# Forgetting attention and SwiGLU FFN on one core: stage-by-stage merged order against an order made by a planner

## Chip, cores and metric

One NeuronCore of one Trainium2 chip. The metric is the device time of one execution in microseconds; the kernel before takes 549.05 us (median of three runs, 547.57 to 549.45).

The engines' short names: PE (TensorE, matmul; PEld its weight loads), DVE (VectorE), ACT (ScalarE), POOL (GpSimd), SP (SyncE, which here only issues DMAs). Each engine executes its own instructions strictly in the order in which the program lists them, and waits on semaphores for the others; so the written order decides what stands behind a wait.

## What is computed

Eight batches, eight heads, 576 tokens, head width 64; then an FFN on all 4608 tokens with model width 512 and hidden width 1536. Everything is float32 outside; the matmuls run in bf16.

```python
def _attn_ref(q, k, v, f):
    scores = (1 / np.sqrt(D)) * q @ k.T              # per batch and head
    cum = np.cumsum(np.log(np.clip(f, 0.0001, 1.0)), axis=-1)
    scores = np.where(causal, -1e9, scores + cum[..., :, None] - cum[..., None, :])
    attn = np.exp(scores - scores.max(-1))
    attn = attn / (attn.sum(-1) + 1e-09)
    return attn @ v

def _moe_ref(x, w_gate, w_val, w_out):               # x: heads side by side
    g = x @ w_gate
    return (g * sigmoid(g) * (x @ w_val)) @ w_out
```

The row term of the decay cancels in the softmax, so the kernel only needs `cum` of the keys.

## The kernel before

**Attention** works on 32 head pairs (two heads of a batch fill the 128 partitions). Queries are cut into nine blocks of 64 tokens; block i sees 64(i+1) keys.

For each pair: `load_pair` (L121) loads q and k on SP's queue so that each packet is one row of 64 elements; q is laid out block-diagonally (zeros in the other head's half), k in six pieces of 96 rows. `cast` (L156) makes bf16 on POOL, `transposes` (L173) turns the nine q and six k pieces with 128-column PE transposes into two PSUM banks `tt`, and DVE copies them out to `kt` and `qz`. `scores` (L205) makes for each block one or two score matmuls (L235), a mask matmul on its last 64 columns (L238), one DVE operation that adds `cb` (the cumulative decay, read back from DRAM for each pair) and finds the minimum (L242), and one ACT exponential that also sums (L247). `normalize` (L253) takes reciprocals on DVE (L261, L262) and multiplies on POOL into a packed bf16 tile `pk` (L267), in three groups of blocks (0 to 3, 4 to 7, 8); a DMA transpose on SP's queue turns each group of `pk` into `pT` (L271). `weighted` (L278) multiplies the values of both heads, as one 128-column weight, with `pT` for both heads (L292): of each result only the half that belongs to the head is copied, by two ACT copies of 64 partitions, from the one PSUM bank `xo` into the ring `xT` (L305). The values come through casting DMAs on POOL's queue (L152), the FFN weights too (L403, L407).

**FFN** works on nine tiles of 512 tokens. A gate unit (`gate`, L312) is four matmuls of 512 columns with `wg` (`gp`), a tanh on ACT (L329), four matmuls with `wv` (`vp`), and two DVE products (L333, L337) into `hh`; twelve of them make a tile. A projection unit (`project`, L341) is twelve matmuls (L349) for 128 tokens, an ACT scaling (L353) and an output DMA. `gp`, `vp` and `op` share three PSUM banks; scores have two, `tt` two, `xo` one.

**Order.** It is written by hand: stage s of 33 merges, by fractions of the stage, the scores of pair s, the weighted sums of pair s - 1, the transposes of pair s + 1, the casts of pair s + 2, the loads of pair s + 3 (`merge`, L359), and from stage five on four FFN units. What is left of the FFN follows after the last stage. In the first stages the weights are loaded at one piece a stage (L399).

Of the kernel before, what the change touches and what calls it, by code (L numbers as in the profile page):

```python
# [8 lines left out]
F32 = mybir.dt.float32  # L9
# [3 lines left out]
AX = mybir.AxisListType  # L13
# [3 lines left out]
HUGE = 3.0e38  # L17


@with_exitstack  # L20
def kernel(
# [16 lines left out]
    P = 128  # L38
# [6 lines left out]
    MT = 512  # L45
    NMT = N_TOK // MT
    scale = 1.0 / (D ** 0.5)
    assert NB * QB == S and D == 64 and NMT * MT == N_TOK
# [5 lines left out]
    GCH = [2, 4, 5]  # L54
    GOFF = [0, 8, 24]
    NSLOT = 29

    ORDER = [8, 4, 5, 6, 7, 0, 1, 2, 3]
    KR, KC = 96, 6
    NRING = 5 * MT  # L60

    consts = ctx.enter_context(tc.tile_pool(name="consts", bufs=1))
    keep = ctx.enter_context(tc.tile_pool(name="keep", bufs=1))
    ldb = ctx.enter_context(tc.tile_pool(name="ldb", bufs=2))
    att = ctx.enter_context(tc.tile_pool(name="att", bufs=2))
    cpool = ctx.enter_context(tc.tile_pool(name="cpool", bufs=2))
    tpool = ctx.enter_context(tc.tile_pool(name="tpool", bufs=3))
    epool = ctx.enter_context(tc.tile_pool(name="epool", bufs=4))
    small = ctx.enter_context(tc.tile_pool(name="small", bufs=4))
    ptpool = ctx.enter_context(tc.tile_pool(name="ptpool", bufs=2))  # L70
    ffn = ctx.enter_context(tc.tile_pool(name="ffn", bufs=2))
    spool = ctx.enter_context(tc.tile_pool(name="spool", bufs=3))
    opool = ctx.enter_context(tc.tile_pool(name="opool", bufs=2))
    ps = ctx.enter_context(tc.tile_pool(name="ps", bufs=1, space=PSUM))


    ident = consts.tile([P, P], BF16)
    make_identity(nc, ident[:, :])


    maskf = consts.tile([P, QB], F32)
# [6 lines left out]
    mask = consts.tile([P, QB], BF16)  # L88
    nc.vector.tensor_copy(mask, maskf)

    xT = consts.tile([P, KD, NRING], BF16)
    wg = consts.tile([P, KD, DF], BF16)
    wv = consts.tile([P, KD, DF], BF16)
    wo = consts.tile([P, KF, DM], BF16)


    qfs, kfs, vts, pks = [], [], [], []
    for n in range(2):
        qf = keep.tile([P, NB, 2, D], F32, name=f"qf{n}")
        nc.vector.memset(qf[0:64, :, 1, :], 0.0)  # L100
        nc.vector.memset(qf[64:128, :, 0, :], 0.0)
        qfs.append(qf)
        kf = keep.tile([P, KC, 2, D], F32, name=f"kf{n}")
        nc.vector.memset(kf[KR:P, :, :, :], 0.0)
        kfs.append(kf)
        vt = keep.tile([P, 5, H, D], BF16, name=f"vt{n}")
        nc.gpsimd.memset(vt[64:128, 4, :, :], 0.0)
        vts.append(vt)

        pk = keep.tile([P, NSLOT, P], BF16, name=f"pk{n}")  # L110
        nc.gpsimd.memset(pk[:, 4:6, :], 0.0)
        nc.gpsimd.memset(pk[:, 20:22, :], 0.0)
        pks.append(pk)

    evs = {}
    for i in range(0, NB, 2):
        ev = keep.tile([P, QB * (i + 2)], F32, name=f"ev{i}")
        nc.gpsimd.memset(ev[:, QB * (i + 1):], 0.0)
        evs[i] = ev

    st = {}  # L121


    def load_pair(p):
        b, hp = divmod(p, NPB)
        qf, kf = qfs[p % 2], kfs[p % 2]

        def lq(h):
            return lambda: nc.sync.dma_start(
                out=qf[64 * h:64 * h + 64, :, h, :],  # L130
                in_=q[b, 2 * hp + h].rearrange("(j r) d -> r j d", r=64),
            )

        def lk(h):
            return lambda: nc.sync.dma_start(
                out=kf[0:KR, :, h, :],
                in_=k[b, 2 * hp + h].rearrange("(c r) d -> r c d", r=KR),
            )
        return [lq(0), lq(1), lk(0), lk(1)]

    def load_cum(p):
        cb = cpool.tile([P, S], F32, name="cb")
        for h in range(2):
            nc.sync.dma_start(
                out=cb[64 * h:64 * h + 64, :],
                in_=cum_dram[2 * p + h:2 * p + h + 1, :].to_broadcast((64, S)),
            )
        st["cb", p] = cb

    def load_v(b, c):  # L150
        n = min(P, S - P * c)
        nc.gpsimd.dma_start(  # L152
            out=vts[b % 2][0:n, c, :, :],
            in_=v[b, :, P * c:P * c + n, :].rearrange("h p d -> p h d"),
        )


    def cast(p):

        def cq():  # L160
            qb = ldb.tile([P, NB, P], BF16, name="qb")
            nc.gpsimd.tensor_scalar(
                qb, qfs[p % 2].rearrange("r j h d -> r j (h d)"), -scale, 1.0,
                op0=ALU.mult, op1=ALU.mult)
            st["qb", p] = qb

        def ck():
            kb = ldb.tile([P, KC, P], BF16, name="kb")
            nc.gpsimd.tensor_copy(kb, kfs[p % 2].rearrange("r j h d -> r j (h d)"))
            st["kb", p] = kb  # L170
        return [cq, ck]

    def transposes(p):  # L173

        def start():
            st["kt", p] = att.tile([P, S], BF16, name="kt")
            st["qz", p] = att.tile([P, NB, P], BF16, name="qz")

        def one(bank, j):
            def f():  # L180
                if j == 0:
                    st["tt"] = ps.tile([P, 8, P], BF16, name="tt", tag="tt", bufs=2)
                tt = st["tt"]
                n = 8 * bank + j
                src = st["kb", p][:, n, :] if n < KC else st["qb", p][:, n - KC, :]
                nc.tensor.transpose(tt[:, j, :], src, ident)  # L186
            return f

        def evac(bank):
            tt = st["tt"]  # L190
            if bank == 0:
                nc.vector.tensor_copy(st["kt", p].rearrange("p (c k) -> p c k", k=KR),
                                      tt[:, 0:KC, 0:KR])
                nc.vector.tensor_copy(st["qz", p][:, 0:2, :], tt[:, KC:8, :])
            else:
                nc.vector.tensor_copy(st["qz", p][:, 2:9, :], tt[:, 0:7, :])

        def both(*fs):
            def f():
                for x in fs:  # L200
                    x()
            return f

        steps = []
        for n in range(15):  # L205
            bank, j = divmod(n, 8)
            fs = [one(bank, j)]
            if n == 0:
                fs.insert(0, start)
            if n in (7, 14):  # L210
                fs.append(lambda bank=bank: evac(bank))
            steps.append(both(*fs))
        return steps

    def scores(p):

        def begin():
            st["tm", p] = small.tile([P, NB + 1], F32, name="tm")
            st["ls", p] = small.tile([P, NB], F32, name="ls")
            st["rl", p] = small.tile([P, NB], F32, name="rl")  # L220

        def block(i):
            def f():
                if i == ORDER[0]:
                    begin()
                kt, qz, cb = st["kt", p], st["qz", p], st["cb", p]
                tm, ls = st["tm", p], st["ls", p]
                L = QB * (i + 1)
                tt = tpool.tile([P, S], F32, name="t")
                n0 = min(L, 512)  # L230
                parts = [(0, n0)] + ([(512, L)] if L > 512 else [])
                for n, (a, z) in enumerate(parts):
                    last = z == L
                    sp = ps.tile([P, 512], F32, name="sp", tag="sp", bufs=2)
                    nc.tensor.matmul(sp[:, :z - a], qz[:, i, :], kt[:, a:z],  # L235
                                     start=True, stop=not last)
                    if last:
                        nc.tensor.matmul(sp[:, z - a - QB:z - a], ident, mask,  # L238
                                         start=False, stop=True)
                    init = HUGE if n == 0 else tm[:, NB:NB + 1]  # L240
                    acc = tm[:, i:i + 1] if last else tm[:, NB:NB + 1]
                    nc.vector.tensor_tensor_reduce(  # L242
                        out=tt[:, a:z], in0=sp[:, :z - a], in1=cb[:, a:z], scale=1.0,
                        scalar=init, op0=ALU.add, op1=ALU.min, accum_out=acc,
                    )
# [6 lines left out]

    def normalize(p, g):  # L253

        i0, i1 = GROUPS[g]
        w = i1 - i0
        pk = pks[p % 2]

# [233 lines left out]
```

## Time and profile before

| what | value |
|---|---|
| median of 3 runs | 549.05 us |
| profiled execution: span from first to last instruction | 546.6 us |
| PE, DVE, ACT, POOL busy | 79%, 64%, 57%, 48% of the span |
| first FFN matmul | 94.2 us |
| start of the last stretch, FFN alone | about 461 us |
| mean granted TensorE clock | 0.928 |

The profile is one execution. "Busy" is the time in which an engine has at least one instruction under way; idle time is put down to what released the engine. A group's row gives its line, engine, operation, output and inputs, shapes, count, busy time, mean duration, and the idle time ahead of it with its releaser. Matmul ends are modelled, so the spacing of starts in a dense run says more of PE's rate than a matmul's duration. A few per cent of matmul records are missing. Shares of DMA time can exceed 1, since packets of a queue overlap.

### The profile page before, as it was taken

What the parts mean: (1) busy time and instruction counts of PE and PEld (TensorE: products, weight loads), DVE (VectorE), ACT (ScalarE), POOL (GpSimd) and SP (SyncE); (2) the same over time, 40 slices, a digit from 0 to 9 for tenths busy, and PEclk for the clock granted to TensorE, in tenths of its full rate; (3) what the DMA queues carried; (4) which work ended last, traced back from release to release, by engine and by line L of the source; (5) the groups of instructions that cost most, each with busy time, mean ns of one, the idle gap of its engine ahead of it and who ended that gap; (6) DMA issues with size and microseconds to landing.
All of it is one profiled execution on the core that took longest, in us unless ns stands there. A gap on an engine that the chain in (4) does not pass through costs nothing.

```text
span 546.6 us, 9410 instructions
## 1 busy us (share of the span) xinstructions
PE 433.7 (79%) x2684; PEld 226.4 (41%) x2736; DVE 352.0 (64%) x1154; ACT 314.0 (57%) x915; POOL 264.1 (48%) x424
## 2 busy tenths in 40 slices
PE   1423516877598888888888888889888988999997
PEld 1312314434344444444444444444444443444443
DVE  6622516767777777777777777777777776454450
ACT  2432626655667766667677667777776766333321
POOL 8561826546655565556555655565556533000000
PEclk9855656989789999999999999999999999999999
DMA  9899999997998999989989989999989754110102
GB/s 140 158 175 147 190 107 181 179 171 137 174 171 170 158 179 149 184 164 153 181 164 164 170 164 165 165 168 168 171 169 171 117 129 117 43 40 38 40 19 96
DMA packets 248403, 78.51 MB, mean 144 GB/s; under 512 B 236960, under 2 KB 238496, under 8 KB 248352
## 3 DMA queue, kind: packets, MB, share of 16 engines
q1 hardware_dynamic: 208096, 68.48, 63.2%
q0 software_dynamic: 40256, 9.44, 19.5%
q8 instruction: 21, 0.34, 0.3%
q14 instruction: 30, 0.25, 0.2%
HBM read 47.33 MB, written 9.58 MB: 104 GB/s over the span
## 4 chain that ended last, share of the span: by engine, by line
PE 56%; DVE 12%; ACT 9%; issue 7%; DMA 7%; POOL 2%; SPq 2%; DVEq 0%; ACTq 0%; POOLq 0%
PE op L349 15%; PE gp L320 13%; PE vp L320 10%; PE xo L292 8%; DMA pT<-pk 6%; PE sp L235 5%; DVE t L242 5%; DVE hh L337 4%; PE tt L186 3%; ACT xT L305 3%; ACT e L247 3%; DVE u L333 2%; ACT th L329 2%; ACT ev L247 2%; PE sp L238 1%
## 5 line engine op out<-in xcount | busy, mean ns | idle before, releaser
L267 POOL TENSOR_SCALAR pk<-ev,rl 128x640 bf16<-128x640 f32 (+4 forms) x160 | 93.0, 581 | 194.3 <-ACT ev L247 73.8
L242 DVE CUSTOM_DVE_ANT_0 t<-sp,cb 128x512 f32<-128x512 f32 (+7 forms) x288 | 134.5, 476 | 80.5 <-PE sp L238 54.2
L292 PE MATMUL xo<-pT,vt 128*128 128x128 bf16 (+2 forms) x348 | 104.4, 304 | 78.0 <-ACT xT L305 46.3
L247 ACT ACTIVATE e<-t,tm 128x384 f32<-128x384 f32 (+3 forms) x128 | 71.3, 557 | 109.1 <-DVE tm L242 62.7
L320 PE MATMUL vp<-xT,wv 128*128 128x512 bf16 x412 | 120.5, 380 | 1.6 <-DVE u L333 0.7
L320 PE MATMUL gp<-xT,wg 128*128 128x512 bf16 x416 | 119.9, 383 | 2.1 <-ACT xT L305 1.6
L333 DVE SCALAR_TENSOR_TENSOR u<-th,gp 128x512 f32<-128x512 f32 x108 | 74.1, 686 | 57.9 <-ACT th L329 57.9
L349 PE MATMUL op<-wo,hh 128*128 128x512 bf16 x420 | 110.2, 379 | 0.4
L247 ACT ACTIVATE ev<-t,tm 128x576 f32<-128x576 f32 (+4 forms) x160 | 89.3, 558 | 33.2 <-DVE tm L242 26.7
L235 PE MATMUL sp<-kt,qz 128*128 128x512 bf16 (+4 forms) x320 | 93.5, 308 | 18.2 <-DVE tm L242 16.6
L329 ACT ACTIVATE th<-gp 128x512 f32<-128x512 f32 x108 | 63.4, 587 | 45.8 <-PE gp L320 38.3
L337 DVE TENSOR_TENSOR hh<-u,vp 128x512 bf16<-128x512 f32 x108 | 74.3, 688 | 11.3
L292 PEld LDWEIGHTS <-vt 128*128 128x128 bf16 x352 | 36.2, 103 | 81.8 <-issue 42.7
L267 POOL TENSOR_SCALAR pk<-e,rl 128x384 bf16<-128x384 f32 (+3 forms) x128 | 67.5, 527 | 0.0
L186 PE MATMUL tt<-ident,qb 128*128 128x128 bf16 x288 | 61.1, 239 | 1.1 <-issue 0.9
L305 ACT CAST xT<-xo 64x256 bf16<-64x256 f32 (+1 forms) x192 | 59.2, 308 | 4.3 <-PE xo L292 2.3
L238 PE MATMUL sp<-mask,ident 128*128 128x64 bf16 x288 | 57.6, 202 | 0.0
L186 PEld LDWEIGHTS <-qb 128*128 128x128 bf16 x288 | 30.5, 108 | 56.2 <-issue 39.0
L235 PEld LDWEIGHTS <-qz 128*128 128x128 bf16 x320 | 33.0, 103 | 40.5 <-issue 9.1
L238 PEld LDWEIGHTS <-ident 128*128 128x128 bf16 x288 | 29.6, 103 | 44.4 <-issue 28.4
L320 PEld LDWEIGHTS <-wg 128*128 128x128 bf16 x432 | 36.1, 98 | 27.3 <-issue 2.8
L320 PEld LDWEIGHTS <-wv 128*128 128x128 bf16 x432 | 35.5, 98 | 24.9 <-issue 8.3
(41 smaller groups left out, 402.2 us busy)
## 6 DMA issues: line engine op xcount, KB each, us to landing
qf<-in_q_dram SPq DMA_DIRECT2D x64, 144.0 KB, 4.4
kf<-in_k_dram SPq DMA_DIRECT2D x64, 144.0 KB, 3.4
cb<-cum_f SPq DMA_DIRECT2D x64, 144.0 KB, 3.6
out_dram<-ot SPq DMA_DIRECT2D x36, 256.0 KB, 2.7
vt<-in_v_dram POOLq DMA_DIRECT2D x32, 128.0 KB, 4.8
pT<-pk SPq DMA_TRANSPOSE x96, 3.9
wg<-in_moe_w_gate_dram POOLq DMA_DIRECT2D x4, 384.0 KB, 9.1
wv<-in_moe_w_val_dram POOLq DMA_DIRECT2D x4, 384.0 KB, 11.0
```

Source lines behind the costliest of these rows:

```text
L186: nc.tensor.transpose(tt[:, j, :], src, ident)
L235: nc.tensor.matmul(sp[:, :z - a], qz[:, i, :], kt[:, a:z], start=True, stop=not last)
L238: nc.tensor.matmul(sp[:, z - a - QB:z - a], ident, mask, start=False, stop=True)
L242: nc.vector.tensor_tensor_reduce(out=tt[:, a:z], in0=sp[:, :z - a], in1=cb[:, a:z], scale=1.0, scalar=init, op0=ALU.add, op1=ALU.min, accu ...
L247: nc.scalar.activation(e[:, :L], tt[:, :L], AF.Exp, bias=tm[:, i:i + 1], scale=-1.0, accum_out=ls[:, i:i + 1])
L267: nc.gpsimd.tensor_scalar(pg[:, 0:m, i - i0, :], e[:, :P * m].rearrange("p (c k) -> p c k", k=P), rl[:, i:i + 1], 1.0, op0=ALU.mult, op1=A ...
L292: nc.tensor.matmul(xo[:, lo * P:w * P], vt[:, c, 2 * hp:2 * hp + 2, :].rearrange("p h d -> p (h d)"), pT[:, c * w + lo:(c + 1) * w, :].rea ...
L305: nc.scalar.copy(dst, xo4[r, :, h, :])
L320: nc.tensor.matmul(st[name], w_[:, ko, fc * P:(fc + 1) * P], xT[:, ko, x0:x0 + MT], start=(ko == 0), stop=(ko == KD - 1))
L333: nc.vector.scalar_tensor_tensor(u, st["th"], 1.0, st["gp"], op0=ALU.add, op1=ALU.mult)
L337: nc.vector.tensor_mul(st["hh", t][:, fc, :], u, st["vp"])
L349: nc.tensor.matmul(op, hh[:, fc, ms * P:(ms + 1) * P], wo[:, fc, :], start=(fc == 0), stop=(fc == KF - 1))
```

## The change

The hand-merged stages are replaced by a planner that runs while the program is built. Every piece of work is declared as an operation: the engines that may do it with a duration for each, what it reads and writes, a priority. `Plan.order` then repeatedly takes the operation that can start first (by priority where several can), gives it a buffer, and moves that engine's clock on; the program is written in order of these starts. Buffers of a ring are given out in order of priority, so that a later user cannot overtake an earlier one. Copies out of PSUM may go to ACT or DVE as the plan finds them free.

Beside the order itself, these things differ:

- q and k: a partition holds 8 (q) or 6 (k) neighbouring rows of a head, so 72 and 96 partitions are used, and a packet is 2 KB or 1.5 KB. Transposes are 72 and 96 columns wide, 14 a pair instead of 15. The copy out of PSUM restores the order of tokens: it reads with a stride and writes `kt` in order; `qz` is written with a stride.
- Weighted sums: two groups (blocks 0 to 3, 4 to 8) instead of three; each key chunk is two matmuls with 64 value columns, one a head, which write partitions 0 to 63 and 64 to 127 of `xo`; one 128-partition copy follows instead of two.
- The packed weights have 25 slots a pair instead of 29. For the first six pairs they are transposed on TensorE, in banks of the FFN's ring (`gv`), and copied by ACT or DVE; the other 26 pairs use the DMA transpose.
- The first four pairs get `cb` by loading the gates with a broadcast and summing them on 128 partitions; the others read `cum_f` back from DRAM. Their groups of blocks 0 to 3 come first, for all four pairs.
- Values are loaded in float32 on SP's queue and cast on POOL. FFN weights come in column cuts (256, 256, 512, 512), each waiting for the one two before it.
- FFN tiles: 256, 256, seven of 512, 256, 256 tokens. In a 256-token tile a PSUM bank holds two hidden chunks. `op` has a bank of its own, `tt` has one instead of two; scores keep two, `xo` one, `gv` three.

The core of the diff:

```diff
+class Plan:
+    def order(self):
...
+        while ready:
+            best = None
+            for n, r in ready.items():
+                o = self.ops[n]
+                got = room(o)
+                if got is None:
+                    continue
+                for e, dur in o.engs.items():
+                    s = max(r, got[0], free[e])
+                    c = (s, o.prio, n, e, dur, got[1])
+                    if best is None or c[:4] < best[:4]:
+                        best = c
...
+            if o.dma:
+                wire = max(wire, free[e] + 600) + o.dma
+                o.end = wire + 1400
+            else:
+                o.end = free[e] + o.lat
...
+        return sorted(done, key=lambda o: (o.start, o.n))
...
-    MT = 512
+    ROWS = {"k": (96, 6), "q": (72, 8)}
+    TILES = [256, 256] + [512] * 7 + [256, 256]
-    GROUPS = [(0, 4), (4, 8), (8, 9)]
+    HI = [3, 8]
+    LO = [0, 4]
+    NSL = [6, 19]
+    ON_PE = {(p, g) for p in range(6) for g in range(2)}
+    ORDER = [(p, g) for g in range(2) for p in range(NPB)]
+    ORDER += [(p, g) for p in range(NPB, NPAIR) for g in (1, 0)]
...
+                in_=src[b, 2 * hp:2 * hp + 2].rearrange("h (p r) d -> p h (r d)", r=ROWS[name][1])),
...
+                for j in range(KC):
+                    nc.tensor.transpose(pl.buf(tk)[:, KR * j:KR * j + KR], src[0:KR, j, :], ident[0:KR, 0:KR])
...
+                    if h is None:
+                        src = pl.buf(tk)[a:z, 0:S].rearrange("r (j p) -> r p j", j=KC)
+                        dst = pl.buf(ok)[a:z, :].rearrange("r (p j) -> r p j", j=KC)
...
+                pl.op({"ACT": 600, "DVE": 680}, evac, [tk] + ([("z", "qz", n) for n in range(5)] if h is not None and p < 5 else []), [ok], s - .9)
...
+            pl.key(bk, "gv" if s < 40 else "tt")
...
+                for h in range(2):
+                    r = slice(64 * h, 64 * h + 64)
+                    nc.tensor.matmul(xo[r, 0:QB * n], vt[:, c, 2 * hp + h, :], pT[:, a:a + n, 64 * h:64 * h + 64],
+                                     start=(c == 0), stop=(c == nch - 1))
...
+        cuts = [0, 256, 512, 1024, 1536]
+        for a, z in zip(cuts, cuts[1:]):
+            for nm, wt, src in (("wg", wg, moe_w_gate), ("wv", wv, moe_w_val)):
+                piece({"POOL": 600}, lambda e, wt=wt, src=src, a=a, z=z: nc.gpsimd.dma_start(
...
+        for u in range(KF // nf):
+            pr = 1000 + t * 20 + u
...
+    with tc.manual_schedule():
+        for o in pl.order():
+            o.fn(o.eng)
```

An attention operation's priority is its place in `ORDER` (0 to 63), an FFN matmul's starts at 1000, and the tanh, products and output copies of the FFN have negative ones.

More of the change, by code (lines that the diff above doesn't have):

```diff
@@ L20, with mm @@
+def mm(*cols):
+    return sum(max(29, c / 2.4 + 2.5) for c in cols)
 @with_exitstack
@@ new lines, with bufs @@
+    cum_dram = nc.dram_tensor("cum_f", (BH, S), F32, kind="Internal").ap()
+    sb = ctx.enter_context(tc.tile_pool(name="sb", bufs=1))
+    ps = ctx.enter_context(tc.tile_pool(name="ps", bufs=1, space=PSUM))
+    pl = Plan()
+    eng = {"DVE": nc.vector, "ACT": nc.scalar, "POOL": nc.gpsimd, "SP": nc.sync}
+    def bufs(name, shape, dtype, n, space=None):
+        pl.pool(name, [(space or sb).tile(shape, dtype, name=f"{name}{x}") for x in range(n)])
+    ident = sb.tile([P, P], BF16)
+    maskf = sb.tile([P, QB], F32)
@@ L173, in transposes @@
[L173 to L235, printed above, removed]
+        s = first[p]
@@ new lines, in epool, with scores, mult @@
+    def epool(i):
+        return f"e{i}" if i % 2 == 0 else "eo"
+    def scores(p, g):
+        s = at[p, g]
+        pl.key(("tm", p, g), "tm")
+        pl.key(("ls", p, g), "ls")
+        for n, bank in enumerate(BANKS[g]):
+            sk = ("sp", p, g, n)
+            pl.key(sk, "sp")
+            pr = s + n * .05
+            def mult(e, bank=bank, sk=sk):
+                sp, kt, qz, o = pl.buf(sk), pl.buf(("kt", p)), pl.buf(("qz", p)), 0
+                for i, a, z in bank:
+                    last = z == QB * (i + 1)
+                    nc.tensor.matmul(sp[:, o:o + z - a], qz[:, i, :, :].rearrange("p h r -> p (h r)"), kt[:, a:z],
@@ L236, in f @@
                                      start=True, stop=not last)
+                    o += z - a
                     if last:
[L238 to L245, printed above, removed]
@@ new lines, in load_v @@
+    def load_v(b):
+        for c in range(5):
+            n = min(P, S - P * c)
+            fk = ("vf", b, c)
+            pl.key(fk, "vf")
+            s = c * .5 - 97 * (c < 2) + 1
+            if b:
+                s = at[b * NPB, 1] + c * .1 - .5
+            wait = [sums[b * NPB - 2 + (c > 2), 0 if b > 1 else 1]] if b else []
+            pl.op({"SP": 620}, lambda e, c=c, n=n, fk=fk: nc.sync.dma_start(
+                out=pl.buf(fk)[0:n, :, :], in_=v[b, :, P * c:P * c + n, :].rearrange("h p d -> p h d")),
+                (), [fk], s, dma=1500 * n / P, after=wait)
+            pl.op({"POOL": 670}, lambda e, c=c, n=n, fk=fk: nc.gpsimd.tensor_copy(pl.buf(("vt", b))[0:n, c, :, :], pl.buf(fk)[0:n, :, :]),
+                  [fk] + [("z", "vt", n_) for n_ in range(2)], [("vt", b), ("vt", b, c)], s + .5)
@@ new lines @@
+    evacs, loads, sums = [], {}, {}
+    for p in range(NPAIR):
+        load_pair(p)
+        prepare(p)
+        for g in range(2):
+            scores(p, g)
+            normalize(p, g)
+            weighted(p, g)
+    for b in range(B):
+        pl.key(("vt", b), "vt")
+        load_v(b)
+    weights()
+    tok, spans = 0, []
+    for t, n in enumerate(TILES):
+        gate(t, tok, n)
+        project(t, tok, n)
+        spans.append((tok, tok + n, t))
+        tok += n
+    for o, (a, z) in evacs:
+        for lo, hi, t in spans:
+            if lo < z - NRING and a - NRING < hi:
+                o.after.append(gates_of[t])
```

639 lines of the change are left out of this document (363 added, 276 removed).

## The prediction

> **What bounds the kernel now.** I read the span and the busy times first, then cut the span where the work changes.
>
> ```profile
> span 546.6 us, 9410 instructions
> PE 433.7 (79%) x2684; PEld 226.4 (41%) x2736; DVE 352.0 (64%) x1154; ACT 314.0 (57%) x915; POOL 264.1 (48%) x424
> ```
>
> The cut comes from the line view of the gate matmuls (first and last start) and the table by stretches; its columns are length, busy time of PE, PEld, DVE, ACT and POOL, granted clock, DMA share, GB/s.
>
> ```profile
> L320 PE MATMUL gp<-xT,wg x416: 376/379/634, 94.2 to 528.7; 128*128 128x512 bf16 x139
> 0.00:94.17 94.17, 36.63 (x230) 23.58 (x234) 41.69 (x157) 37.15 (x114) 52.65 (x92) 0.66 1.07 156
> 94.17:461.00 366.83, 316.38 (x2086) 166.07 (x2127) 272.96 (x943) 250.72 (x756) 209.77 (x329) 0.98 0.93 162
> 461.00:546.60 85.60, 80.69 (x371) 36.71 (x378) 37.33 (x56) 26.18 (x48) 1.63 (x5) 1.00 0.15 53
> ```
>
> There are three regimes. Until 94.2 us no FFN matmul exists: PE is busy 36.6 us at a clock of 0.66, and no compute engine is busy for 60% of it. From there to 461 us attention and FFN run together at full clock, PE busy 86%. After 461 us only FFN is left, PE dense. The chain of waits names the first stretch's limiter, and the list of waits the second's:
>
> ```profile
> 33.56 14.57 DMA pT<-pk
> 67.16 14.82 DMA pT<-pk
> PE xo L292 <- DMA pT<-pk: 31.5, 6, 10.5
> PE xo L292 <- ACT xT L305: 46.3, 40, 1.7
> ```
>
> Two DMA transposes of the packed weights sit on the chain for 14.6 and 14.8 us, both in the stretch where the FFN weights are loaded and the DMA share is above 1. Later PE's commonest wait is the single xo bank, held until ScalarE has copied it out.
>
> One period of the middle stretch (one head pair, three gate units and one projection) and the dense FFN rate:
>
> ```profile
> 179.14:192.52 13.38, 11.82 (x81) 6.25 (x81) 10.12 (x35) 9.30 (x29) 7.72 (x13) 1.00 1.02 168
> 475.54 2.59 PE op L349 x12
> ```
>
> Twelve 512-column matmuls in 2.59 us are 0.4216 ns a column. A period has 36 of these and 8,576 attention columns (1,920 in transposes, 2,880 in scores, 576 of mask, 3,200 in xo), so 27,008 columns or 11.39 us. PE is busy 11.82 us, 0.43 us more for small matmuls, and idle 1.56 us. PE is the bound of two stretches, a DMA wait of the first.
>
> **The change, term 1: the time to the first gate matmul.** In the changed instruction order the first gate stands behind 437 attention matmuls; on ScalarE the first tanh stands behind the exponentials of 6.5 pairs. The FFN's PSUM ring is also used for transposing the first six pairs' weights on TensorE, and buffers are given in order of priority, so the FFN cannot pass them. These pairs no longer meet the DMA transpose, whose 14.6 and 14.8 us waits so go; their price lands on ScalarE, the fullest engine here:
>
> ```profile
> L247 ACT ACTIVATE e<-t,tm 128x384 f32<-128x384 f32 (+3 forms) x128 | 71.3, 557 | 109.1 <-DVE tm L242 62.7
> L247 ACT ACTIVATE ev<-t,tm 128x576 f32<-128x576 f32 (+4 forms) x160 | 89.3, 558 | 33.2 <-DVE tm L242 26.7
> L247 ACT ACTIVATION_READ_ACCUMULATOR ev<-t,tm 128x1 f32 x160 | 30.0, 187 | 0.0
> L247 ACT ACTIVATION_READ_ACCUMULATOR e<-t,tm 128x1 f32 x128 | 23.9, 187 | 0.0
> L329 ACT ACTIVATE th<-gp 128x512 f32<-128x512 f32 x108 | 63.4, 587 | 45.8 <-PE gp L320 38.3
> L353 ACT ACTIVATE ot<-op 128x512 f32<-128x512 f32 x36 | 21.5, 597 | 31.5 <-PE op L349 30.9
> L305 ACT CAST xT<-xo 64x256 bf16<-64x256 f32 x128 | 46.4, 362 | 3.8 <-PE xo L292 2.3
> L305 ACT CAST xT<-xo 64x64 bf16<-64x64 f32 x64 | 12.8, 200 | 0.5
> L384 ACT ACT_TABLE_LOAD x1 | 1.3, 1283 | 0.7 <-PEq L476 0.7
> L384 ACT ACTIVATE t<-t 64x576 f32<-64x576 f32 x1 | 0.7, 682 | 4.9 <-DVE t L383 4.9
> 5.43 1.43 DVE L383 TENSOR_SCALAR t<-t 64x576 f32<-64x576 f32 x1
> L192 DVE COPY kt<-tt 128x576 bf16<-128x576 bf16 x32 | 15.4, 481 | 15.6 <-PE tt L186 15.6
> L162 POOL TENSOR_SCALAR qb<-qf 128x1152 bf16<-128x1152 f32 x32 | 36.9, 1153 | 2.8 <-DMA qf<-in_q_dram 2.1 <-DVE kf L104 0.7
> ```
>
> Exponentials and their accumulator reads cost (71.3+89.3+30.0+23.9)/32 = 6.70 us a pair. With three tanh (1.76), one ot (0.60) and xT ((46.4+12.8)/32 = 1.85) a period's rows sum to 10.91 us, where ScalarE is busy 9.30: rows overlap, and 0.853 turns them into occupied time, 5.72 us a pair, 37.2 for 6.5 pairs. Copies out of PSUM follow the two xT rows: 162 ns for 192 columns, 0.844 ns a column, and 146 ns fixed. Thirteen pT copies of 9,472 columns are 9.9 us. Six k or q copies of 576 columns are 0.63 each, 3.8 (their strided source has no row: the DVE copy of that size, 0.48, bounds it below, the cast qb of 1,152 elements, 1.15, above: 2.9 to 6.9; 0.63 because the xT rows are this engine reading PSUM). Five logarithms 3.4, six table loads 7.7 (the logs of later pairs stand between exponentials, two loads before), five xT copies 2.0, one cast of q 1.0 (between the same 1.15 and 0.63). Sum 65.0 us. The clip shows when the forget gates reach an engine, 5.4 us; I take 5, and for the rest the best utilization that a bound engine shows here, PE's 11.82/13.38 = 0.883: 73.6. First gate at **78 us** where it was 94; bounds 70 (ScalarE never waits) and 94 (no gain).
>
> The forget gates of four pairs are now broadcast from the input and summed on 128 partitions, so the first scores don't wait for cum_f to go out and return; that adds four clips and scans to DVE, which is as full as ScalarE here:
>
> ```profile
> L333 DVE SCALAR_TENSOR_TENSOR u<-th,gp 128x512 f32<-128x512 f32 x108 | 74.1, 686 | 57.9 <-ACT th L329 57.9
> L337 DVE TENSOR_TENSOR hh<-u,vp 128x512 bf16<-128x512 f32 x108 | 74.3, 688 | 11.3
> L388 DVE TENSOR_TENSOR_SCAN t<-t 64x576 f32<-64x576 f32 x1 | 1.4, 1350 | 0.1
> 0.74 0.58 SPq L381 DMA_DIRECT2D t<-in_f_dram  x1
> ```
>
> A period's DVE time, 10.12, less three u and hh (4.12) is 6.0; on 6.5 pairs 39, five clips and scans 14, eleven pT copies at about 0.7 (one u row) 8, ten memsets 3: 64 us. The first f, k, q and V loads alternate on SP's queue at some 0.6 us an issue; its first transpose stands behind 46 loads, so none of them waits for a pack.
>
> **Term 2: PE after the first gate.** FFN: 663,552 columns, as before, 279.8 us. The 256-token tiles at both ends issue 384 matmuls of 256 columns; each at 108 ns still covers a weight load of 98 ns (row below), so nothing, and 8 us at 0.02 each if not.
>
> ```profile
> L320 PEld LDWEIGHTS <-wg 128*128 128x128 bf16 x432 | 36.1, 98 | 27.3 <-issue 2.8
> ```
>
> Attention after the first gate: 204,800 columns. The q and k transposes shrink from 1,920 to 1,152 columns a pair (96 and 72 neighbouring rows, no padding). xo keeps its 3,200, but as pairs of 64-column weights writing disjoint partition halves. The trace has no such matmul. Bounds: one after the other, 86.3 us; together, less half of 89,600 xo columns, 18.9 us, gives **67.4**. I take together, since within each pair operands and outputs are independent and nothing else in the array waits; the other end stays in the range.
>
> The rule that speaks against: the Trainium skill, "TensorEngine Tiling (Array Packing)", Key Properties and Restrictions, says that tiles run independently, yet that changing the mode drains the array and that column tiling switches fast weight load off. The first would make it 67 us, the second puts a price on each of the 128 switches that this order has; no row before shows either.
>
> Small matmuls: 0.43 us a pair on 25.5 pairs, **11**. Idle: 1.56 us a pair before. Of that the xo bank's 46.3/32 = 1.45 now has two turns a pair instead of three, and one 128-partition copy of about 0.42 us on either of two engines instead of two of 0.36 in turn on one: 1.45 x 2/3 x 0.42/0.72 = 0.56. What is late next is tt, cut from two banks to one, and held through each copy: I add 0.34, together 0.9 a pair, **23** us; bounds 0 and the 1.56 of before, 0 and 40.
>
> **Term 3: behind the last matmul**, as before:
>
> ```profile
> 542.97 0.60 ACT L353 ACTIVATE ot<-op 128x512 f32<-128x512 f32 x1 [1.99 <-PE op L349]
> ```
>
> 546.6 - 543.0 = **3.6** us.
>
> **What is priced at nothing, and its cover.** DMA: q and k go from 73,728 packets of one 64-element row to 10,752 longer ones, and the packed slots from 29 to 25 a pair; V keeps its packets but moves to SP's queue and gets a cast on POOL (under 1.15 us, the larger q cast), which replaces L152's issues there. Queue row:
>
> ```profile
> q1 hardware_dynamic: 208096, 68.48, 63.2%
> L152 POOL DMA_DIRECT2D vt<-in_v_dram x40 | 35.4, 888 | 0.0
> ```
>
> Cover: two buffers each of pk, pT and vt. If it goes, PE meets pT as in the 31.5 us row. VectorE: the adds, products and normalization keep their columns, the copies are shared with ScalarE; its 352 us stays within some 10. Of 362, 64 lie before the first gate and 33 in a tail of 75 us (37.33/85.60 of it, as now), so 265 remain for the 306 us between, 87%, against 10.12/13.38 = 76% now: thin cover, see the second rival.
>
> **Sum:** 78 + 280 + 67 + 11 + 23 + 3.6 = 463 us of span. The median is 549.05 against a span of 546.6, 2.4 more: **465 us**.
>
> **Rivals.**
> (a) *Column halves cost more.* No overlap adds 18.9 (484). A drained array adds, per switch, what a lone matmul shows over its slot:
>
> ```profile
> L292 PE MATMUL xo<-pT,vt 128*128 128x512 bf16 x124 | 50.6, 408 | 71.6 <-ACT xT L305 40.0 <-DMA pT<-pk 31.5
> ```
>
> 408 - 216 = 192 ns, two switches for each of 56 groups: 21.5 us. Both: 505. For: 64 bursts; against: FFN's independent matmuls follow at once. (The Trainium skill, "TensorEngine Tiling (Array Packing)", Key Properties, has the mode change as its rule.)
> (b) *VectorE becomes the bound* and cannot pass 76%: 265/0.756 = 350 us between first gate and the FFN tail (75 us of columns stand behind the last xo): 78+350+75+3.6+2.4 = 509. For: nothing before shows DVE fuller. Against: it was never what PE waited for most.
> (c) *The stalls nearly vanish*: first gate at 70, small matmuls 6, idle 8: 437.
> (d) *Slower.* SP's queue holds loads, transposes and outputs in one written order; a 19-slot transpose whose pack is late holds the next loads behind it, and xo cannot start. It decides once a pair takes over (549-78-75-6)/25.5 = 15.3 us; landing like the two 14.6 and 14.8 us transposes plus a 0.4 us xo matmul and its copy would do: 555. For: DMA share is 0.93 in the middle now. Against: those two fell among weight loads, which now are all issued before the first DMA transpose.
> (e) *The start does not shorten*, as ScalarE, VectorE and POOL, each near full there, wait for one another in turn: 465 + 16 = 481. For: in the first 94 us ScalarE is busy 37 us now. Against: that stretch's long waits were the two transposes.
>
> **How the numbers follow.** Forecast 0.53 (own range 447 to 479), (a) 0.15, (b) 0.11, (c) 0.10, (e) 0.06, (d) 0.05. The range runs from (c)'s upper part past (a)'s full price: 440 to 506; some 0.2 lies outside. A difference under 0.3% can't be told from none here; faster 0.94, within 0.3% 0.01, slower 0.05.
>
> **What would show it.** First gate matmul near 78 us, ScalarE above 80% busy before it; a steady pair period of about 11.5 us with PE idle near 0.9; xo pairs starting together; some 75 us of dense FFN at the end; no pT wait over 5 us. Wrong if xo's two halves start one after the other, if PE waits for DVE at most places, or if pT returns to the chain.

## The result and the profile after

The changed kernel takes 465.22 us (median of 4 runs, 464.1 to 466.25) against 549.12 us of the kernel before beside it: ratio 0.847, 95% interval 0.844 to 0.850. The forecast was 465 us. That the number is met does not say that its terms are: two of them were off by some 11 and 17 us, in opposite directions, and that they cancel is luck.

First the page's span and busy times of the changed kernel, the gate matmuls' line (first and last start), and the table by stretches, cut at the first gate and at the last xo (length, busy PE, PEld, DVE, ACT, POOL, clock, DMA share, GB/s):

```profile
span 462.3 us, 9695 instructions
PE 412.8 (89%) x3093; PEld 231.5 (50%) x3142; DVE 358.8 (78%) x1106; ACT 300.0 (65%) x815; POOL 255.6 (55%) x456
...
L539 PE MATMUL gv<-xT,wg x518: 272/379/391, 89.4 to 447.6; 128*128 128x512 bf16 x109, 128*128 128x256 bf16 x64
...
0.00:89.40 89.40, 49.69 (x436) 33.66 (x439) 65.02 (x206) 60.41 (x153) 62.68 (x117) 0.85 0.93 179
89.40:381.00 291.60, 287.68 (x2226) 154.61 (x2263) 259.31 (x851) 216.57 (x624) 192.90 (x340) 1.00 0.92 187
381.00:462.30 81.30, 75.44 (x436) 43.25 (x444) 34.52 (x51) 23.06 (x39) 0.00 (x0) 0.99 0.11 43
```

The three stretches are there again. The first is hardly shorter (89.4 against 94.2 us), but holds more attention than before. In the second PE is busy 287.7 of 291.6 us, 98.7%, where it was 86%; VectorE is at 89%. The last is dense FFN. PE's total busy time fell by 21 us, the rest of the 84 us is idle time that has gone.

The waits on the xo bank, PE's longest before, have turned round. These are lines of the list of waits after: the copies wait for PE.

```profile
PE sp L369 <- DVE qz L350: 11.4, 6, 2.8
...
ACT xT L483 <- PE xo L465: 7.6, 9, 1.8
...
DVE xT L483 <- PE xo L465: 4.6, 10, 1.0
```

The span closes with the last output copy, seen in the timeline:

```profile
458.41 0.60 ACT L572 ACTIVATE ot<-op 128x512 f32<-128x512 f32 x1 [2.89 <-PE op L563]
```

### The profile page after: what moved, and what is told of

The parts are those of the page before. It is cut to its first block, busy times and chain, and to the rows that moved or that the text cites. A ratio compares the mean times of both kernels' runs of the same rounds, so it can differ in the third digit from the quotient of the medians.

```text
span 462.3 us, 9695 instructions
## 1 busy us (share of the span) xinstructions
PE 412.8 (89%) x3093; PEld 231.5 (50%) x3142; DVE 358.8 (78%) x1106; ACT 300.0 (65%) x815; POOL 255.6 (55%) x456
## 2 busy tenths in 40 slices
DMA packets 150338, 74.12 MB, mean 160 GB/s; under 512 B 125072, under 2 KB 136848, under 8 KB 150288
## 3 DMA queue, kind: packets, MB, share of 16 engines
q0 software_dynamic: 5808, 4.72, 6.9%
## 4 chain that ended last, share of the span: by engine, by line
PE 74%; DVE 9%; DMA 5%; POOL 5%; ACT 3%; issue 3%; SPq 1%; another core or an unknown queue 0%; ACTq 0%; POOLq 0%; DVEq 0%
PE gv L539 36%; PE op L563 18%; PE sp L369 8%; PE xo L465 5%; POOL pk L423 3%; DVE t L385 3%; PE tt L334 3%; DMA vf<-in_v_dram 2%; DVE qz L350 2%; DMA qf<-in_q_dram 2%; PE gv L442 2%; PE sp L373 1%; DMA kf<-in_k_dram 1%; DVE th L547 1%; ACT eo L399 1%
## 5 line engine op out<-in xcount | busy, mean ns | idle before, releaser
L423 POOL TENSOR_SCALAR pk<-e,ls 128x512 bf16<-128x512 f32 (+1 forms) x192 | 102.8, 539 | 93.4 <-DVE tm L385 32.9
L539 PE MATMUL gv<-xT,wg 128*128 128x512 bf16 (+1 forms) x518 | 109.9, 340 | 0.6
L539 PE MATMUL gv<-xT,wv 128*128 128x512 bf16 (+1 forms) x517 | 109.5, 340 | 0.6 <-DVE th L547 0.2
L399 ACT ACTIVATE e<-t,tm 128x448 f32<-128x448 f32 (+4 forms) x160 | 88.5, 554 | 32.6 <-DVE tm L385 31.0
L547 DVE SCALAR_TENSOR_TENSOR th<-th,gv 128x512 f32<-128x512 f32 x108 | 73.7, 683 | 40.7 <-ACT th L545 40.2
L545 ACT ACTIVATE th<-gv 128x512 f32<-128x512 f32 x108 | 63.8, 591 | 58.3 <-PE gv L539 57.6
L369 PE MATMUL sp<-kt,qz 128*128 128x128 bf16 (+6 forms) x316 | 75.7, 306 | 20.8 <-DVE qz L350 11.4
L550 DVE TENSOR_TENSOR hh<-th,gv 128x512 bf16<-128x512 f32 x108 | 72.9, 683 | 10.8 <-PE op L563 4.8
L423 POOL TENSOR_SCALAR pk<-eo,ls 128x256 bf16<-128x256 f32 (+3 forms) x128 | 68.5, 536 | 11.5 <-DVE ls L410 8.6
L399 ACT ACTIVATE eo<-t,tm 128x256 f32<-128x256 f32 (+3 forms) x128 | 70.7, 553 | 3.7 <-DVE tm L385 3.0
```

The lines of the kernel that those rows point to most:

```text
L369: nc.tensor.matmul(sp[:, o:o + z - a], qz[:, i, :, :].rearrange("p h r -> p (h r)"), kt[:, a:z], start=True, stop=not last)
L399: nc.scalar.activation(pl.buf(ek)[:, :L], pl.buf(tk)[:, :L], AF.Exp, bias=pl.buf(("tm", p, g))[:, i:i + 1], scale=-1.0, accum_out=pl.buf(( ...
L423: nc.gpsimd.tensor_scalar(dst, src, pl.buf(("ls", p, g))[:, i:i + 1], 1.0, op0=ALU.mult, op1=ALU.mult)
L539: nc.tensor.matmul(pl.buf(bk)[:, j * n:j * n + n], wt[:, ko, fc * P:fc * P + P], xT[:, ko, x0:x0 + n], start=ko == 0, stop=ko == KD - 1)
L545: pl.op({"ACT": 487}, lambda e, u=u: nc.scalar.activation(pl.buf(("th", t, u)), pl.buf(("wg", t, u)), AF.Tanh, scale=0.5), [("wg", t, u)], ...
L547: pl.op({"DVE": 605}, lambda e, u=u: nc.vector.scalar_tensor_tensor(pl.buf(("th", t, u)), pl.buf(("th", t, u)), 1.0, pl.buf(("wg", t, u)), ...
```

## The experiments

Every run is the changed kernel with one edit, and its order is planned anew. Runs are compared with 465.2 us; the median of the kernel before beside them was 545.6 to 548.6 us. The changed kernel was not run again beside them, and the kernel before moved by 0.6% from set to set (549.1 against 545.6 us), so a difference of 2 or 3 us is weak evidence. "First gate" is the first start of a gate matmul (89.4 us in the changed kernel).

### The written order

Planner told that every operation takes 500 ns:

```diff
+        engs, lat = {e: 500 for e in engs}, 100
         o = Op(len(self.ops), engs, fn, list(reads), list(writes), prio, lat, dma, list(after), holds)
```

> The planner believes that every operation takes 500 ns on its engine and is visible 100 ns later; DMA times, priorities, buffers and the work stay. Theory (PE is 98.7% busy from the first gate to the last xo because the written order fits the real durations): PE idle there returns to the share of before, about 14% or 40 us, 490 to 515 us. Rival (the rings and the lower demand do it, the order needs no good durations): 464 to 475 us.

Measured: 506.99 us (506.86 to 507.87), 41.8 us slower, a total that the first theory forecast. The first gate moved only to 91.7 us. From about there to 426 us (the last xo starts at 434.9), this run's table by stretches:

```profile
90.00:426.00 336.00, 309.49 (x2269) 166.44 (x2307) 250.66 (x823) 236.66 (x664) 194.01 (x336) 0.98 0.80 162
```

PE is idle for 26.5 us there instead of 3.9. Over the whole run it is idle 30 us longer and busy 13 us longer (425.6 against 412.8). The idle share there, 8%, is not back at the 14% of before, so rings and lighter work do their part; but half of the gain of the change hangs on the planner's durations being near the real ones. The idle time did not come back where it was. Two of PE's waits, over the whole run (its lines are numbered one higher):

```profile
PE sp L370 <- DVE tm L386: 12.4, 28, 1.4
PE xo L466 <- ACT xT L484: 0.8, 2, 0.5
```

PE now waits for VectorE to free the score banks and, for some 7 us in that stretch, for the single output bank; hardly ever for xo, which was 46.3 us before the change. No run keeps the hand-merged order with the rest of the change, so the order and the lighter work are not fully told apart.

### The column halves

```diff
-            for c in range(nch):
-                for h in range(2):
+            for h in range(2):
+                for c in range(nch):
...
```

> The ten or four xo matmuls of a burst are issued all for the first head and then all for the second, so neighbours use the same column half; nothing else changes. Theory (the halves run side by side in the changed kernel): a burst of ten should take 2,432 columns x 0.4216 = 1.03 us to the next matmul's start instead of the 0.64 us seen at 249.97 us, a burst of four 0.32 instead of 0.29; 0.42 us a pair on 25.5 pairs behind the first gate, where PE is 98.7% busy: 11 us slower, 474 to 478 us. Rival (they run one after the other anyway): 464 to 467 us.

Measured: 470.01 us (468.62 to 471.56), 4.8 us slower. A burst of ten with its neighbours, on PE's timeline of the changed kernel:

```profile
249.66 0.38 PE L539 MATMUL gv<-xT,wv 128*128 128x512 bf16 x1
249.97 0.71 PE L465 MATMUL xo<-pT,vt 128*64 128x320 bf16 x10
250.61 0.39 PE L369 MATMUL sp<-kt,qz 128*128 128x512 bf16 x1
```

and of this run:

```profile
251.93 0.87 PE L465 MATMUL xo<-pT,vt 128*64 128x320 bf16 x10
252.74 0.39 PE L369 MATMUL sp<-kt,qz 128*128 128x512 bf16 x1
```

From the burst's start to the next matmul's it is 0.64 us against 0.81. The table by stretches of 0.02 us for this line alone (count in brackets) shows the starts: in the changed kernel

```profile
249.95:249.97 0.02, 0.00 (x1) 0.00 (x1) 1.00 0.97 230
249.97:249.99 0.02, 0.02 (x2) 0.02 (x2) 1.00 0.88 269
```

two matmuls are under way almost at once; issued in turn, the first is alone for more than 0.12 us:

```profile
251.92:251.94 0.02, 0.01 (x1) 0.01 (x1) 1.00 1.89 499
252.04:252.06 0.02, 0.02 (x1) 0.02 (x1) 1.00 0.86 231
252.08:252.10 0.02, 0.02 (x3) 0.01 (x2) 1.00 0.48 115
```

So the halves do run side by side. The run's price fits: 28 of the 32 ten-bursts lie behind the first gate, and 0.17 us on each is 4.8 us. The 11 us expected was too much, because even in turn a burst doesn't take the 1.03 us that its columns come to at the full-width rate. The reason is in this run's lines by shape from 251.93 to 252.33 us:

```profile
L465 PE MATMUL xo<-pT,vt 128*64 128x320 bf16 x5 | 0.6, 309 | 0.0
```

Five matmuls of 320 columns have started and none of 192, although the first head has only three of 320 and its 192-column one is written ahead of all of the second head's. So PE started the second head's matmuls before the first head's were through, some 0.17 us behind them: between the two column halves the written order did not hold, so the strict order that the start of this document gives every engine has an exception here.

### The transposes of the first pairs

```diff
-    ON_PE = {(p, g) for p in range(6) for g in range(2)}
+    ON_PE = set()
```

> No pair's packed weights are transposed on TensorE; all 32 pairs use the DMA transpose, and the order is planned anew. Theory (what the six pairs save is the 14.6 and 14.8 us that a DMA transpose took amid the weight loads): the first gate is free of the ring and may come before 75 us, but waits for pT of 5 us and more return in the first 100 us and the total is 470 to 485 us. Rival (the six pairs only trade a DMA for copies on ScalarE and VectorE): 458 to 467 us, no pT wait over 3 us.

Measured: 485.2 us (483.49 to 485.82), 20 us slower, though its first gate comes at 52.2 us. Its chain of waits (start, length):

```profile
47.70 21.72 DMA pT<-pk
...
77.88 12.17 DMA pT<-pk
...
91.92 9.65 DMA pT<-pk
```

and its stretch 52.2 to 130 us, where PE is busy 70%:

```profile
52.20:130.00 77.80, 54.38 (x448) 38.10 (x453) 44.54 (x147) 41.74 (x115) 44.95 (x75) 0.82 1.16 201
```

Long waits for the DMA transpose are back. In this run the DMA transposes begin at 30 us, and the weight loads are issued until 94 us; in the changed kernel the last weight load is issued at 76.9 us and the first DMA transpose at 96.5 us. The six pairs' PE transposes are what keeps the two apart, and an early first gate alone gains nothing here.

```diff
-    ON_PE = {(p, g) for p in range(6) for g in range(2)}
+    ON_PE = {(p, g) for p in range(4) for g in range(2)}
```

> Pairs 4 and 5 use the DMA transpose like those behind them, so the first gate stands behind the exponentials of 4 pairs instead of 6.7. Theory (the reserved ring of the FFN holds the first gate back, and behind it PE is the bound): first gate at 55 to 65 us, 2.5 pairs of attention (8 us of PE) move behind it: 440 to 452 us. Rival (behind the gate VectorE, 89% busy there, or DMA transposes amid the weight loads become the bound): 458 to 470 us.

Measured: 467.21 us (466.33 to 467.79): a miss for the theory, and within the rival's range. The first gate does come at 64.6 us, yet:

```profile
0.00:64.60 64.60, 33.05 (x292) 21.80 (x293) 44.03 (x134) 44.35 (x103) 43.81 (x87) 0.93 0.92 179
64.60:89.40 24.80, 24.04 (x240) 19.20 (x238) 22.91 (x73) 17.89 (x51) 14.16 (x24) 0.97 1.04 171
89.40:389.90 300.50, 286.34 (x2151) 146.09 (x2149) 254.51 (x843) 215.86 (x627) 197.44 (x348) 0.98 0.92 190
```

By 89.4 us PE has done 57.1 us of work instead of 49.7. Then it is idle for 14.2 us instead of 3.9, and the last xo comes at 389.9 us instead of 381. FFN work done early is missing later, while PE waits for attention. PE's longest waits of this run between 64.6 and 390 us:

```profile
PE sp L369 <- DVE qz L350: 3.4, 4, 1.5
PE tt L334 <- ACT kt L348: 2.8, 1, 2.8
PE sp L369 <- ACT qz L348: 2.8, 4, 1.0
```

With 1.5 us for `kt` on VectorE, 10.5 us are waits for the copies of q and k out of PSUM; none of the listed waits is for a DMA transpose. So PE is not the only bound behind the first gate. Whether those copies are late for VectorE and ScalarE themselves or for what stands ahead of them was not separated.

### Loads

```diff
-        cuts = [0, 256, 512, 1024, 1536]
+        cuts = [0, 256]
...
-        for c in range(0, KF, 4):
+        for c in range(0, 4, 4):
```

> Only the first 256 columns of wg and wv and the first 512 rows of wo are loaded and all gate and projection matmuls read these, so the result is not the reference's and 3.5 MB of the 4.7 MB of weight traffic is gone; all compute instructions stay. Theory A (the first gate at 89.4 instead of 78 us is late because weight traffic delays q, k and V in the first 75 us): first gate at 76 to 80 us, total 452 to 457 us. Theory B (ScalarE, VectorE and POOL wait for each other in the written order, whatever the DMAs do): first gate at 87 to 91, total 463 to 467 us.

Measured: 460.18 us (459.76 to 461.26), first gate at 86.2 us: between the two theories. The matmuls read the loaded pieces in place of the missing ones, so their number stays. The weights left out (POOL's queue moves 1.05 MB instead of 4.72) go with about 3 us of the start and 5 us in all, not the 11 us that were to be explained.

q and k by rows of 64 elements (core; the cast reads the matching order):

```diff
...
-                in_=src[b, 2 * hp:2 * hp + 2].rearrange("h (p r) d -> p h (r d)", r=ROWS[name][1])),
+                in_=src[b, 2 * hp:2 * hp + 2].rearrange("h (p r) d -> p r h d", r=ROWS[name][1])),
```

> q and k are read so that each packet is one row of 64 elements again (73,728 packets instead of 10,752); the rows of a partition, all casts, transposes and copies stay. Theory (packet count is covered, as the prediction priced it, by the buffers ahead of each pair): 464 to 470 us. Rival (DMA time is the next bound in the middle, where its share is 0.92): 63,000 more packets at some 25 ns over 16 queues are 98 us of DMA time, 3 us a pair, and the middle of 292 us grows with it: 480 to 505 us, with waits for kf or qf or pT on PE or POOL.

Measured: 466.89 us (465.2 to 466.98). The page of this run, its DMA line:

```profile
DMA packets 213315, 74.12 MB, mean 159 GB/s; under 512 B 198801, under 2 KB 204433, under 8 KB 213265
```

The changed kernel has 150,338 packets. The 63,000 more cost nothing that can be told: the longer packets are no visible part of the gain.

V by casting DMAs again:

```diff
...
-            pl.op({"SP": 620}, lambda e, c=c, n=n, fk=fk: nc.sync.dma_start(
-                out=pl.buf(fk)[0:n, :, :], in_=v[b, :, P * c:P * c + n, :].rearrange("h p d -> p h d")),
+            pl.op({"POOL": 900}, lambda e, c=c, n=n: nc.gpsimd.dma_start(
+                out=pl.buf(("vt", b))[0:n, c, :, :], in_=v[b, :, P * c:P * c + n, :].rearrange("h p d -> p h d")),
```

> V goes back to casting DMAs on POOL's queue, straight into vt, without a float32 tile and without the cast on POOL. Theory (in the first 75 us POOL's casts of V wait for their loads with the packing queued behind them, and hold the first gate back): first gate at 80 to 85 us, 457 to 461 us. Rival 1 (V is not what holds it): 463 to 467 us. Rival 2 (casting DMAs hold POOL 0.89 us each, longer than the 0.62 us cast, and slow the queues): 468 to 475 us.

Measured: 468.75 us (468.57 to 469.23), first gate at 91.4 us: the second rival. Loading V in float32 and casting it on POOL is worth some 3.5 us, and is not what makes the start long.

### Tiles and free copies

```diff
-    TILES = [256, 256] + [512] * 7 + [256, 256]
+    TILES = [512] * 9
```

> Nine tiles of 512 tokens, nothing else. The prediction priced the 256-token tiles at nothing: 464 to 467 us. Rival 1 (their 256-column matmuls cost 0.02 us more each): 456 to 459 us. Rival 2 (they let the FFN start or end earlier): 468 to 474 us, to be seen in the first gate's time or in the last stretch.

Measured: 464.27 us (462.23 to 464.82). No difference: the 256-token tiles are priced right at nothing.

```diff
-                pl.op({"ACT": 600, "DVE": 680}, evac, [tk] + ([("z", "qz", n) for n in range(5)] if h is not None and p < 5 else []), [ok], s - .9)
+                pl.op({"DVE": 680}, evac, [tk] + ([("z", "qz", n) for n in range(5)] if h is not None and p < 5 else []), [ok], s - .9)
...
-            o = pl.op({"ACT": QB * (z - a) * .833 + 130, "DVE": QB * (z - a) / .96 + 85}, evac, [xk],
+            o = pl.op({"ACT": QB * (z - a) * .833 + 130}, evac, [xk],
...
-            pl.op({"ACT": 495, "DVE": 620}, evac, [bk], [ok], pr - 5000)
+            pl.op({"ACT": 495}, evac, [bk], [ok], pr - 5000)
```

> Copies out of PSUM lose their free choice: k and q copies only on VectorE, xT and output copies only on ScalarE, as before the change; the pT copies of the first six pairs stay free. VectorE gains 52 copies of about 0.75 us and loses 46 of 0.42 to 0.69: some 15 us more of DVE work in a stretch where it is 89% busy. Theory (rival b of the prediction is close: cover is thin): 472 to 485 us with VectorE over 90% busy before the last xo. Rival (PE alone sets the time): 464 to 468 us.

Measured: 466.11 us (463.87 to 466.19): the rival. Its middle stretch:

```profile
90.70:381.00 290.30, 289.31 (x2256) 155.80 (x2255) 270.80 (x852) 205.92 (x619) 193.55 (x339) 1.00 0.92 188
```

VectorE is driven to 270.8 of 290.3 us, 93%, and PE still is busy 99.7%. The choice of engine for a copy gains nothing that can be told here, and 76% was no limit of VectorE.

### What the start waits for

```diff
...
-              P, -100 + 3 * p)
+              P, -100 + p * .1 + (p > 0) * 1.2)
...
-    gates("fa", [(0, BH, fall)], BH, -100 + 3 * NDIRECT)
+    gates("fa", [(0, BH, fall)], BH, -98)
...
-                          pr, lat=150, holds=[("tm", p, g)])
+                          pr, lat=150, holds=[("tm", p, g)], after=lns if (p, g) == (0, 0) else [])
```

(`lns` is the list of the gates' logarithms, so that the first exponential of the attention waits for all of them.)

> All forget gates are loaded and their logarithms taken before the first exponential: two activation table loads instead of six in the start, 5.1 us less on ScalarE, and four instructions of the start move ahead. Theory A (ScalarE's work sets the first gate, as the prediction priced it): first gate at 83 to 85 us instead of 89.4, total 458 to 462 us. Theory B (the limit is a chain through POOL and VectorE): first gate at 88 to 91 us and 464 to 468.

Measured: 464.47 us (463.32 to 467.57), first gate at 85.4 us, but with 404 instead of 437 attention matmuls ahead of it. The gate's time lies between the two theories, with less work ahead of it. The wide spread and the unchanged total leave theory A without support.

```diff
             engs = {"POOL": 850}
+            if p < 6:
+                engs = {"POOL": 850, "ACT": 900}
```

> The q and k casts of pairs 1 to 5 may be planned on POOL or ScalarE; five of the ten go to ScalarE ahead of the first gate, about 5 us of work from POOL to ScalarE. Theory A (ScalarE sets the start): first gate 3 to 5 us later, 468 to 471 us. Theory B (POOL, 62.7 us busy of the first 89.4 and not priced by the prediction, sets it): first gate at 83 to 86 us, 459 to 462 us.

Measured: 460.32 us (460.12 to 460.7), first gate at 84.6 us behind the same 437 matmuls: theory B. Its first stretch:

```profile
0.00:84.60 84.60, 48.54 (x438) 33.02 (x439) 66.14 (x215) 62.87 (x156) 57.93 (x111) 0.90 0.97 189
```

4.8 us of work have left POOL, ScalarE has 2.5 us more, and the first gate comes 4.8 us earlier. This is the fastest of the versions that load all the weights: about 1% under the changed kernel by the medians, and the runs of the two don't overlap.

With that edit kept, the casts of V's first two batches free between POOL and ScalarE as well:

```diff
-            pl.op({"POOL": 670}, lambda e, c=c, n=n, fk=fk: nc.gpsimd.tensor_copy(pl.buf(("vt", b))[0:n, c, :, :], pl.buf(fk)[0:n, :, :]),
+            pl.op({"POOL": 670, "ACT": 600} if b < 2 else {"POOL": 670}, lambda e, c=c, n=n, fk=fk: (nc.scalar.copy if e == "ACT" else nc.gpsimd.tensor_copy)(pl.buf(("vt", b))[0:n, c, :, :], pl.buf(fk)[0:n, :, :]),
```

> As the run with the free q and k casts, and the V casts of the first two batches may be planned on ScalarE too; two of them, 1.2 us, leave POOL ahead of the first gate. Theory (POOL's work sets the start): first gate at 82 to 84.5 us, 457 to 460 us. Rival (ScalarE is now as full as POOL there and the gain is used up): first gate at 84.5 to 87, 460 to 463 us.

Measured: 462.45 us (461.92 to 463.43), first gate at 85.5 us: the rival, and 2.1 us slower than the run before it. Its first stretch:

```profile
0.00:85.50 85.50, 48.95 (x437) 33.59 (x438) 64.29 (x211) 62.14 (x154) 58.90 (x112) 0.86 0.96 186
```

POOL's 58.9 us are no less than the 57.9 of the run before it: two of V's casts went to ScalarE, two of the q and k casts came back to POOL, and nothing more is gained. Whether a start with clearly less work on POOL would be shorter still was not tried.

One rival to POOL was not tested: the clock granted to TensorE before the first gate. It was 0.85 in the changed kernel, 0.90 with the free q and k casts and 0.91 with few weights. Between runs of one kernel it points both ways: with nine tiles of 512, one run at a mean clock of 0.978 took 462.2 us and three at 0.967 took 464.0 to 464.8; with the logarithms first, the one run at 0.978 took 467.6 us and three at 0.970 took 463.3 to 464.5. So it stays open how much of the 4.9 and 5.0 us goes with the clock.

## Why the prediction was right, point by point

**First gate: 78 us forecast, 89.4 measured.** This term failed. Its work was sized well: ScalarE 65.0 us forecast and 60.4 measured, VectorE 64 and 65.0. The step that failed is the utilization: 0.883 was carried over from PE, as if ScalarE alone set the stretch; ScalarE was busy 68% of it, where the prediction's sign was above 80%. POOL's 62.7 us had not been added up at all. Three engines with 60 to 65 us each hand work round in a circle (exponential, normalization, packing, transpose, copy), and each reached only about 70%; that the circle is the reason is argued, not shown. These are rival (e)'s terms: 481 less 465 was its price, 11 of the 16 us came. That POOL is part of the limit is made likely by the five casts moved off it, which came with 4.8 us; weight traffic has some 3 us in it, both with the clock as a rival; V's loads and ScalarE's table loads were not shown to have any. The rest stays open.

**PE's work behind it: 358 us forecast (280 + 67 + 11), 363 measured** (287.7 + 75.4). The overlap was right in kind and mis-sized. From its start to the next matmul a burst of ten takes 0.64 us and one of four 0.29. Ahead of it, from the start of a 512-column matmul to the burst's start, pass 0.31 us (249.66 to 249.97) where the next full-width matmul follows after 0.22; in the kernel before, with 128 weight columns, that step to xo took 0.22 us too where it waited for nothing. With 0.09 us for each of its two steps a pair costs 1.12 us, against 1.35 for its 3,200 columns at the full rate and 0.67 for half of them. On the 28 pairs behind the first gate that is 31.3 us where 18.9 were forecast: of the 18.9 us to be saved, 6.5 came. That PE's sum is only 5 us off is luck again: for the small matmuls some 3.5 us are left instead of 11 (363.1 less 279.8 of FFN, 48.5 of other attention and 31.3), a rough figure, as some matmul records are missing.

**Idle: 23 us forecast, 5.8 measured**, 3.9 of it up to the last xo and 1.9 behind it. Here the prediction scaled the wait on the xo bank by turns and copy lengths. But the wait was one of order: in the trace of the changed kernel at least 0.74 us of other matmuls lie between any two bursts behind the first gate, and the copy takes 0.35 to 0.49 us, so the single bank costs nothing, and tt's single bank (0.34 us a pair assumed) hardly more. The run with equal durations puts 22.6 us of idle time back, but at other places; its wait for xo stays at 0.8 us. So the size of the idle time hangs on the durations, while xo's wait is gone in both orders. Rival (c)'s "stalls nearly vanish" is what happened to this term.

**End: 3.6 us forecast, 3.9 measured** (458.4 to 462.3).

The sum held because 11 us too little at the start and 5 too little on PE met 17 too much in the idle time: 89.4 + 363.1 + 5.8 + 3.9 = 462.2.

**Priced at nothing:** packets of q and k, and the 256-token tiles, right by their own runs. V's move was worth 3.5 us. The copies of k and q, 0.63 us each in the forecast, are 0.63 on ScalarE and 0.75 on VectorE:

```profile
L348 ACT COPY kt<-tt 128x576 bf16<-128x576 bf16 x22 | 13.8, 629 | 8.0 <-PE tt L334 7.9
L350 DVE COPY kt<-tt 128x576 bf16<-128x576 bf16 x10 | 7.5, 752 | 1.2 <-PE tt L334 1.1
```

**Rivals.** (a) came in part. The halves overlap; but a burst costs about 0.22 us more than half its columns: 0.13 from its start on (0.64 against 0.51, 0.29 against 0.16) and 0.09 ahead of it. The rival's two drains of 0.192 us are 0.38; on 56 bursts the 0.22 us are 12.4 us, where it forecast 21.5. So of the two rules of the Trainium skill's "TensorEngine Tiling (Array Packing)", Key Properties, the independence of tiles is seen in the starts, and a change of mode may be what the 0.22 us is; no run separates it. (b) fell: 89% was reached between the first gate and the last xo, and 93% in the run with the copies fixed. (d) fell: between 100 and 381 us the chain of waits of the changed kernel has no DMA transpose among its pieces.

## What to carry to other kernels

Here a stall behind a single buffer was a matter of what the order put beside the copy: price such a stall from the work that could stand there, not from the copy's length. Where three engines share a stretch in a circle, add up the work of all of them, and don't expect from each the utilization of an engine that others merely feed. A planner's order is as good as its durations: with made-up ones it lost 42 of the 84 us.

## What was not expected of the hardware

Ten matmuls of 64 weight columns, issued one half after the other, took 0.81 us for 2,432 columns, 0.33 ns a column, where full-width matmuls took 0.42: halves overlap in part even when their issue is not paired, because PE starts the second half's matmuls ahead of ones written earlier. Going from 128 to 64 weight columns and back costs time on both sides: 0.09 us ahead of a burst, and behind it 0.12 us from the start of the last 64-column matmul to the next, where a 64-column matmul between full-width ones takes 0.03. With VectorE at 93% and PE at 99.7% VectorE's copies of kt took no longer than in the changed kernel, where VectorE was at 89%: 749 ns against 752, as the group of the run with VectorE alone copying shows:

```profile
L350 DVE COPY kt<-tt 128x576 bf16<-128x576 bf16 x32 | 24.0, 749 | 0.3 <-PE tt L334 0.3
```
